# New due times for a planner's order, and short identity matmuls among TensorE's waits

## The chip, the core and the metric

The kernel runs on one core of a Trainium2 chip. The metric is the device time of one execution in microseconds (us). A core has five engines, each with an instruction queue of its own: TensorE (PE in the profile; its weight loads are PEld), VectorE (DVE), ScalarE (ACT), GpSimd (POOL) and SyncE (SP), which issues most transfers. Matmuls write their results to PSUM, a memory of 8 banks with 512 floats per partition; the other tiles lie in SBUF. Engines wait for each other by semaphores.

## What is computed

Attention for 4 batches of 8 heads, 1152 keys of 64 dimensions and 576 pooled queries, and behind it a feed-forward layer with a SoLU activation for 2304 tokens.

```python
def _attn_ref(q, k, v) -> np.ndarray:
    B, H, S, D = q.shape
    factor = 2
    scale = 1.0 / np.sqrt(D)
    q_pool = q.reshape(B, H, S // factor, factor, D).mean(axis=3)
    scores = scale * np.matmul(q_pool, k.transpose(0, 1, 3, 2))
    scores = scores - np.max(scores, axis=-1, keepdims=True)
    attn = np.exp(scores)
    attn = attn / (np.sum(attn, axis=-1, keepdims=True) + 1e-09)
    return np.matmul(attn, v).astype(np.float32)
...
def _moe_ref(x, w_in, w_out, g_ln) -> np.ndarray:
    h = x @ w_in
    h_max = np.max(h, axis=-1, keepdims=True)
    e = np.exp(h - h_max)
    sm = e / (np.sum(e, axis=-1, keepdims=True) + 1e-09)
    solu = h * sm
    mu = np.mean(solu, axis=-1, keepdims=True)
    var = np.mean((solu - mu) ** 2, axis=-1, keepdims=True)
    ln = (solu - mu) / np.sqrt(var + 1e-06) * g_ln
    return (ln @ w_out).astype(np.float32)
```

## The kernel before

The heads are worked through in pairs. For a pair, keys and queries are loaded, scaled, split into a high and a low f16 part and transposed by DMA (tiles `kn`, `qa`, `qb` before, `w`, `q` behind the transposition; L733 and L837). Small copies follow: `khi` and `w2h` take the keys into other partitions (L738, L1102), and `zq` takes the last 64 queries of both heads of a pair side by side (L843).

For each head, `maxima` first multiplies queries with keys on TensorE (`bank<-w,q`, and for the last queries `bank<-khi,zq`); VectorE takes the maximum of each row (`mx`, L977 and L982). TensorE transposes the maxima, and a transfer puts them as an additional row under the queries (`q<-c`, L1003). Then `scores` multiplies keys with queries again, now transposed and with the maximum subtracted (`bank<-q,w` and `bank<-q,w2h`), ScalarE takes the exponential (`e`, `eh`, `er`; L1133, L1139, L1150), GpSimd or VectorE forms what is left of it after rounding to f16 (L1160, L1166), and TensorE multiplies it with the values (`bank<-vhi,eh`, `bank<-vlo,eh`, in some steps `bank<-vx,eh` in f32). The sums of one head lie in bank 7 of PSUM, in its columns 0 to 324. When a head is through, VectorE copies and adds a part of them (L1224, L1228), takes the reciprocal of the row sums (L1231, L1239) and divides (L1242), which frees the bank.

The feed-forward layer takes 128 tokens at a time, in 18 blocks: `bank<-wb,xt` is its first product, `bank<-wb,lt` its second. Its weights come as float64 and are put together from bytes in the first 230 us (tile `raw`, L535; `up`, L544; `wb`, L554). Blocks of a batch can start when its 8 heads are through, so the last blocks follow the last head.

No order is written out. Every operation is given to a planner, `Plan.add`, with its engine, an estimated length, a due time and what it reads and writes. The due time is a number from the loops plus an offset from the table `OFF`, looked up by the tile's name and its head, pair or block. `Plan.run` plays all engines with these lengths: whenever an engine is free it takes, among the operations whose inputs and buffers are there, the one with the earliest due time. The program is then written out in the order of these played starts. On the chip only this order is left; the times are those of the chip, and an engine whose next instruction waits does nothing else. In the first 20 us matmuls of an f32 identity (L1639, `plan.warm`) stand between the first matmuls, where the played TensorE has nothing to do.

Of the kernel before, what the change touches and what calls it, by code (L numbers as in the profile page):

```python
# [22 lines left out]
KP = {'W': [5, 5.2, 61, 4.1], 'step': 1.05, 'M': [78.33, 15.88, 7.65], 'TX': 118, 'TP': 69, 'win': 4.28, 'P': [24.74, 18.81, 12.81, 18.34, 35, 22.83], 'QP': 29, 'N': [11.98, 7], 'AV': 5.18, 'CD': [[27, 53, 2], [69, 288, 10]], 'SD': [[12, 83, 5], [70, 287, 1]], 'VM': 'BCCCBCCCBCCBCCCB', 'OF': [4.76, 1.62, 9.84, 2.47, 1.86], 'N1': 8.51, 'warm': 1, 'ws': -3.83, 'GR': 0, 'GG': 13, 'b_eh': 6, 'b_w1': 4, 'V0': -98.83, 'VF': 1, 'QD': [0, 1], 'L0': 2.74, 'F': 0, 'EX': [[10, 71, 33], [42, 282, 0]], 'LX': [3, 36.19], 'HP': [146073, 0], 'DL': 2000, 'MA': 18.0, 'TR': [2000, 2], 'P1': [-3.89, -3.14, 3.71, -7.84, -10.1, 0.03], 'WS': [54, 96, 0.22], 'KD': 5.48, 'RB': [0, 1], 'XE': 3, 'ZB': 7, 'LT': 16, 'RS': [2.5, 6.5], 'LO': 0.3, 'PD': [], 'KH': [1], 'ZE': [2, 8], 'VN': 4}  # L23
# [19 lines left out]
class Plan:  # L43
# [20 lines left out]
    def __init__(self, tags, banks, window):  # L64
        self.tags, self.banks, self.window = tags, banks, window
        self.bank, self.slot = {}, {}
        self.warm, self.warm_until = None, 0
        self.ops = []
        self.parts, self.writers, self.readers = defaultdict(dict), {}, defaultdict(list)
        self.users = defaultdict(int)  # L70
# [53 lines left out]
    def run(self):  # L124
        ops = self.ops
# [20 lines left out]
        kind, dma, extra = "", 0, []  # L146
# [63 lines left out]
        while events:  # L210
            t, what, _, arg = heapq.heappop(events)
            if what == 0:
                o, done = arg, done + 1
                for b in o.uses:
                    count[b] -= 1
                    for i in where[b]:
                        last[i][o.engine] = o
                    if not count[b]:
                        for i in where[b]:
                            held[i] = None  # L220
                        for e in ready:
                            push(t, 1, e)
                for m in after[o]:
                    e = m.engine
                    hop = self.HOP[o.engine][e] + (self.LOAD[m.kind] if e == "PE" != o.engine else 0)
                    if o.engine == e and not m.deps[o]:
                        hop = 0
                    elif e == "PE" != o.engine and t > PAD[0]:
                        hop += pad
                    m.ok_at = max(m.ok_at, t + hop)  # L230
                    m.left -= 1
                    if not m.left:
                        ready[e].append(m)
                        push(m.ok_at, 1, e)
                continue
            e = arg
            if busy[e] > t:
                continue
            best = None
            limit = 1e9 if not todo else now_mark + (self.window if todo < len(marks) else FIRST)  # L240
            for o in ready[e]:
                if o.at > limit or o.ok_at > t or (best is not None and (o.at, o.n) >= (best.at, best.n)):
                    continue
                g = buffers(o)
                if g is None:
                    continue
                s = could(o, g)
                if s > t:
                    push(s, 1, e)
                    continue  # L250
                best, got = o, g
            if best is None:
                if e == "PE" and self.warm and t > KP.get("ws", 2.5) * 1000 and todo > self.warm_until:
                    i = next((i for i in range(8) if held.get(i) is None), None)
                    if i is not None:
                        extra.append((t, lambda i=i: self.warm(i)))
                        busy[e] = t + (110 if t > self.COLD else 216)
                        push(busy[e], 1, e)
                continue
            o = best  # L260
            ready[e].remove(o)
            for b, c in got.items():
                where[b] = c
                before[b] = [x for i in c for x in last[i].values()]
                for i in c:
                    held[i] = b
                    last[i] = {}
                if b[0] in self.banks:
                    self.bank[b] = c
                else:  # L270
                    turn[self.tags[b[0]][0]] += 1
                    self.slot[b] = c[0][1]
                head[b[0]] += 1
            for d in (*o.deps, *(x for b in o.uses for x in before.get(b, ()))):
                known[e][d.engine] = max(known[e][d.engine], d.rank)
            o.start, o.rank = t, ranks[e]
            ranks[e] += 1
            length = o.length
            if e == "PE":
                length += self.SWITCH.get((kind, o.kind), 0)  # L280
                kind = o.kind
                length *= 1 if t > self.COLD else 2
            if e == "SP":
                early = t < 4000
                busy[e] = t + (450 if early else 640) * o.calls
                dma = max(dma, t + 1200) + length
                o.end = dma + (800 if early else KP.get("DL", 1000))
            else:
                begin = t
                if o.port and e == "DVE":  # L290
                    begin = max(t, busy["POOL"] - 190)
                    taken_until = begin + length
                elif o.port and e == "POOL":
                    begin = max(t, taken_until)
                busy[e] = o.end = begin + length
            if o.mark is not None:
                todo -= 1
                if o.mark > now_mark or not todo:
                    now_mark = o.mark
            for x in ready:  # L300
                push(t, 1, x)
            push(o.end, 0, o)
            push(busy[e], 1, e)
        if done < len(ops):
            raise ValueError([(o.n, o.engine, o.at, o.uses, o.left) for o in ops if o.start is None][:30])
        self.end = max(busy.values())
        calls = [(o.start, o.n, o.fn) for o in ops] + [(t, -1, fn) for t, fn in extra]
        for _, _, fn in sorted(calls, key=lambda x: x[:2]):
            fn()


def MM(n, c=1):
    return c * (n / 2.26 + 6.5)


def MH(n, c=1):
    return c * (n / 2.4 + 2.8)

# [22 lines left out]
def attention_solu_moe(  # L341
# [10 lines left out]
    nc = tc.nc  # L352
# [28 lines left out]
    OF = KP.get("OF", [5, 1.5, 10, 1, 1.5])  # L381
    TP, TX = KP.get("TP", 90), KP.get("TX", 100)
# [54 lines left out]
    plan = Plan(tags, banks, window=KP.get("win", 5))  # L437
# [37 lines left out]
    def flat(t):  # L475
        return t.rearrange("p a b -> p (a b)")
# [5 lines left out]
    bank = pp.tile([128, 8, 512], F32, name="bank")  # L482
    ident = const.tile([128, 128], F32, name="ident")
    id16 = const.tile([128, 128], F16, name="id16")
    idb = const.tile([128, 2, 128], BF16, name="idb")
    wb = [const.tile([128, 9, WN], F32, name=f"wb{i}") for i in range(2)]
    w16 = [t.rearrange("p n c -> p (n c)").bitcast(F16).rearrange("p (n r c) -> p n r c", n=9, r=2) for t in wb]
    wm = [const.tile([128, 8], F32, name=f"wm{i}") for i in range(2)]
    ws = [const.tile([128, 16], F32, name=f"ws{i}") for i in range(2)]
    gc = const.tile([128, KO], F32, name="gc")  # L490
    xs = const.tile([128, B + B // 2, 8], F32, name="xs")
# [3 lines left out]
    vx = [const.tile([128, 2, NJ, D + 1], F32, name=f"vx{i}") for i in range(2)]  # L495
# [5 lines left out]
    mz = const.tile([128, 5, D + 1], F32, name="mz")  # L501
# [1066 lines left out]
    with tc.manual_schedule():  # L1568
# [59 lines left out]
        def token_job(n, at, src, key, dsts, rate, tail, x):  # L1628
            prev[0] = tokens(n, src, key, dsts, at, rate, prev[0], tail, x)

        for n, (x, r, tail, src, key, dsts) in enumerate(toks):
            t = max(t, r)
            jobs.append((t, lambda n=n, t=t, s=src, k=key, d=dsts, tail=tail, x=x: token_job(n, t, s, k, d, MR, tail, x)))
            t += MP if n > 4 else KP.get("MA", MP)
        jobs.append((t + 100, lambda: prev[0](t)))
        for _, job in sorted(jobs, key=lambda x: x[0]):
            job()
        if KP.get("warm", 12):
            plan.warm = lambda i: nc.tensor.transpose(bank[:, i, 0:128], ident, ident)  # L1639
            plan.warm_until = NS + 2 * NJ - 2 * KP.get("warm", 12)  # L1640
        plan.run()


# [1 line left out]
_INS = ["q", "k", "v", "moe_w_in", "moe_w_out", "moe_g_ln"]  # L1645


# [23 lines left out]
```

## Time and profile before

| | us |
|---|---|
| median of 3 runs | 624.45 (622.62 to 626.06) |
| the profiled execution | 630.24 |
| its span, first to last instruction | 628.4 |
| PE busy | 594.5 (95%) |
| ACT busy | 506.7 (81%) |
| DVE busy | 505.1 (80%) |
| POOL busy | 469.0 (75%) |
| mean granted clock of TensorE | 0.98 |

The profile is of one execution. A row of it names the engine, the source line, the operation and its tiles, output before input, with buffer numbers left out. Most matmuls have the line of a helper (L463), so they are told apart by their tiles. The granted clock is a share of full speed, averaged over a stretch. The profiled execution is not one of the three that give the median.

### The profile page before, as it was taken

What the parts mean: (1) busy time and instruction counts of PE and PEld (TensorE: products, weight loads), DVE (VectorE), ACT (ScalarE), POOL (GpSimd) and SP (SyncE); (2) the same over time, 40 slices, a digit from 0 to 9 for tenths busy, and PEclk for the clock granted to TensorE, in tenths of its full rate; (3) what the DMA queues carried; (4) which work ended last, traced back from release to release, by engine and by line L of the source; (5) the groups of instructions that cost most, each with busy time, mean ns of one, the idle gap of its engine ahead of it and who ended that gap; (6) DMA issues with size and microseconds to landing.
All of it is one profiled execution on the core that took longest, in us unless ns stands there. A gap on an engine that the chain in (4) does not pass through costs nothing.

```text
span 628.4 us, 17256 instructions
## 1 busy us (share of the span) xinstructions
PE 594.5 (95%) x6630; PEld 368.2 (59%) x6635; DVE 505.1 (80%) x1189; ACT 506.7 (81%) x978; POOL 469.0 (75%) x491
## 2 busy tenths in 40 slices
PE   8978989998888899999999999999999999999997
PEld 6747666765545465565665556556566666654453
DVE  6966788989799998878977999888989887529460
ACT  5866787998889889888998798898989989946361
POOL 5796666665777889898899889788999989932130
PEclk9996979999899899999999999999999999999999
DMA  9183967387987658767748679767697453146322
GB/s 262 35 177 98 205 179 165 75 189 154 187 225 149 133 103 182 150 151 128 142 76 144 158 142 189 139 148 111 129 164 133 81 103 79 29 67 117 69 50 68
DMA packets 183790, 83.00 MB, mean 132 GB/s; under 512 B 168604, under 2 KB 169372, under 8 KB 183708
## 3 DMA queue, kind: packets, MB, share of 16 engines
q1 hardware_dynamic: 183196, 81.18, 63.5%
q8 instruction: 52, 0.85, 0.6%
q10 hardware_dynamic: 512, 0.72, 0.3%
q14 instruction: 30, 0.25, 0.1%
HBM read 36.70 MB, written 4.72 MB: 66 GB/s over the span
## 4 chain that ended last, share of the span: by engine, by line
PE 71%; DVE 16%; ACT 4%; POOL 2%; DMA 2%; issue 2%; SPq 1%; DVEq 0%; POOLq 0%; ACTq 0%
PE bank L463 68%; DVE mx L982 6%; POOL eh L1160 2%; PE bank L1639 1%; ACT e L1139 1%; DMA zq<-q 1%; DVE wb L473 1%; DVE kn L473 1%; DVE eh L1153 1%; DVE mx L977 1%; ACT eh L1139 1%; DMA q<-c 1%; DVE ln L1459 1%; PE bank L743 1%; DVE wb L554 1%
## 5 line engine op out<-in xcount | busy, mean ns | idle before, releaser
L1160 POOL TENSOR_TENSOR eh<-e,eh 128x512 f16<-128x512 f32 (+1 forms) x278 | 331.7, 1212 | 65.2 <-ACT e L1139 24.0
L982 DVE TENSOR_REDUCE mx<-bank 128x1 f32<-128x512 f32 (+1 forms) x300 | 188.0, 653 | 25.5 <-PE bank L463 24.5
L463 PEld LDWEIGHTS <-eh 128*128 128x128 f16 x3246 | 137.9, 99 | 66.0 <-issue 9.5
L1139 ACT ACTIVATE e<-bank 128x512 f32<-128x512 f32 (+1 forms) x259 | 154.0, 614 | 24.6 <-POOL eh L1160 11.6
L1139 ACT ACTIVATE eh<-bank 128x512 f16<-128x512 f32 (+3 forms) x257 | 151.6, 616 | 27.5 <-PE bank L463 26.1
L463 PE MATMUL bank<-vhi,eh 128*128 128x65 f16 x2159 | 149.8, 196 | 7.1 <-DVE x L1242 3.0
L463 PE MATMUL bank<-q,w 128*128 128x64 f16 (+2 forms) x612 | 142.5, 294 | 6.1 <-ACT e L1139 2.2
L463 PE MATMUL bank<-q,w2h 65*128 65x512 f16 (+1 forms) x540 | 127.3, 288 | 0.0
L463 PE MATMUL bank<-w,q 128*128 128x512 f16 (+2 forms) x390 | 109.1, 339 | 4.2 <-DVE mx L982 2.6
L463 PE MATMUL bank<-wb,xt 128*128 128x512 f16 x432 | 113.0, 379 | 0.0
L463 PE MATMUL bank<-wb,lt 128*128 128x512 f16 x432 | 110.5, 379 | 0.1
L463 PE MATMUL bank<-vlo,eh 128*128 128x64 f16 x1087 | 104.5, 195 | 0.0
L463 PEld LDWEIGHTS <-w2h 65*128 65x128 f16 x540 | 45.2, 98 | 32.4 <-issue 9.3
L463 PEld LDWEIGHTS <-w 128*128 128x128 f16 x540 | 46.6, 98 | 23.9 <-issue 2.2
L463 PEld LDWEIGHTS <-lt 128*128 128x128 f16 x432 | 38.8, 98 | 37.0 <-issue 0.4
L463 PEld LDWEIGHTS <-xt 128*128 128x128 f16 x432 | 38.0, 98 | 36.5 <-issue 2.6
L1166 POOL TENSOR_TENSOR er<-r,er 128x320 f16<-128x320 f32 (+1 forms) x60 | 51.3, 857 | 8.7 <-ACT er L1150 5.0
L463 PEld LDWEIGHTS <-q 128*128 128x128 f16 x360 | 31.3, 99 | 21.1 <-issue 3.6
L1360 DVE TENSOR_REDUCE st<-bank 128x1 f32<-128x512 f32 x36 | 24.3, 682 | 21.3 <-PE bank L463 21.3
L1384 ACT ACTIVATE e<-bank,st,xs 128x512 f32<-128x512 f32 x36 | 27.7, 777 | 14.9 <-DVE st L1363 9.8
L1422 POOL TENSOR_TENSOR st<-st 128x1 f32<-128x1 f32 x18 | 4.3, 239 | 38.4 <-DVE st L1411 36.8
L1150 ACT ACTIVATE r<-bank 128x320 f32<-128x320 f32 (+1 forms) x60 | 25.6, 431 | 4.0 <-PE bank L463 3.8
(143 smaller groups left out, 900.8 us busy)
## 6 DMA issues: line engine op xcount, KB each, us to landing
vx<-in_v_dram SPq DMA_DIRECT2D x32, 288.0 KB
kt<-in_k_dram SPq DMA_DIRECT2D x31, 288.0 KB
qt<-in_q_dram SPq DMA_DIRECT2D x15, 576.0 KB
out_dram<-o SPq DMA_DIRECT2D x35, 128.0 KB
khi<-w SPq DMA_DIRECT2D x30, 144.0 KB
w2h<-w SPq DMA_DIRECT2D x30, 144.0 KB
raw<-in_moe_w_in_dram SPq DMA_DIRECT2D x8, 511.6 KB
raw<-in_moe_w_out_dram SPq DMA_DIRECT2D x8, 511.6 KB
```

Source lines behind the costliest of these rows:

```text
L463: nc.tensor.matmul(out=o, lhsT=a, rhs=b, start=first, stop=last, skip_group_check=True)
L473: eng.scalar_tensor_tensor(out=o, in0=a, scalar=scale, in1=b, op0=ALU.mult, op1=ALU.subtract)
L554: nc.vector.scalar_tensor_tensor(out=w32.bitcast(I32), in0=tl["raw", n][:, :, 0], scalar=5, in1=tl["wps", n].bitcast(I32), op0=ALU.logical ...
L743: nc.tensor.transpose(ps[:, c, :], tl["kt", 0][:, h, 3 * i + c, :], ident)
L977: nc.vector.tensor_reduce(out=tl["mx", g][:, 0:4, 2], in_=tl["nps", (g, m, c)], op=ALU.max, axis=AXX)
L982: nc.vector.tensor_reduce(out=tl["mx", g][:, m, c:c + 1], in_=tl["nps", (g, m, c)], op=ALU.max, axis=AXX)
L1139: nc.scalar.activation(out=o if P else o.rearrange("p (f i) -> p f i", f=2), in_=i, func=ACTF.Exp, scale=esc)
L1150: nc.scalar.activation(out=o, in_=tl[rn(u), (g, u)], func=ACTF.Exp, scale=esc)
L1160: eng.tensor_tensor(out=e[:, o:o + c.stop - c.start], in0=e32[:, c], in1=e[:, c], op=ALU.subtract)
L1166: eng.tensor_tensor(out=e[:, :, 1, :], in0=tl["r32", (g, u)][:, 0:len(RU[u]), :], in1=e[:, :, 0, :], op=ALU.subtract)
L1360: nc.vector.tensor_reduce(out=st(f), in_=tl[H_[f]], op=ALU.max, axis=AXX)
L1384: nc.scalar.activation(out=tl[E][:, f * 512:(f + 1) * 512], in_=tl[H_[f]], func=ACTF.Exp, bias=st(2), scale=xs[:, r, 3:4], accum_out=st(3 ...
```

## The change

Three things change. The table `OFF` has new numbers throughout (some 700), made anew with a planner that takes TensorE at half rate behind spans in which it has little to do; the planner in the kernel itself plays no such rate. The other entries of `KP` stay, and `KW` is added. A new function, `idle`, looks at the played starts between 23 and 250 us: it finds gaps of more than 350 ns between TensorE's operations, leaves out those in which bank 7 belongs to something else than a head's sums, and fills up to six tenths of a gap with matmuls at 80 ns each until the played TensorE is busy enough by the numbers of `KW`. Such a matmul (`plan.keep`) multiplies the identity in bf16 with 184 columns of itself into columns 328 to 511 of bank 7, which nobody reads. One more stands near the beginning and starts the accumulation.

```diff
-KP = {'W': [5, 5.2, 61, 4.1],
+KP = {'KW': [0.55, 0.6, 250000, 23000], 'W': [5, 5.2, 61, 4.1],
...
-OFF = {'am.0': 28.38, 'am.1': -49.32, 'am.10': 1.42,
+OFF = {'am.0': -39.66, 'am.1': -70.36, 'am.10': -7.68,
...
 FIRST = KP.get("L0", 0.3)
+KEEP = 7
@@ -65,6 +66,7 @@
         self.tags, self.banks, self.window = tags, banks, window
         self.bank, self.slot = {}, {}
         self.warm, self.warm_until = None, 0
+        self.keep, self.turns = None, []
         self.ops = []
         self.parts, self.writers, self.readers = defaultdict(dict), {}, defaultdict(list)
         self.users = defaultdict(int)
@@ -267,6 +269,8 @@
                     last[i] = {}
                 if b[0] in self.banks:
                     self.bank[b] = c
+                    if KEEP in c:
+                        self.turns.append((t, b[0] == "av"))
                 else:
                     turn[self.tags[b[0]][0]] += 1
                     self.slot[b] = c[0][1]
@@ -304,9 +308,33 @@
         if done < len(ops):
             raise ValueError([(o.n, o.engine, o.at, o.uses, o.left) for o in ops if o.start is None][:30])
         self.end = max(busy.values())
+        if self.keep:
+            extra += self.idle()
         calls = [(o.start, o.n, o.fn) for o in ops] + [(t, -1, fn) for t, fn in extra]
         for _, _, fn in sorted(calls, key=lambda x: x[:2]):
             fn()
+
+    def idle(self):
+
+        pe = sorted((o.start, o.end, 0.5 if o.kind in ("whole", "round") else 1.0) for o in self.ops if o.engine == "PE")
+        want, share, until, begin, span = *KP["KW"], 3413
+        gaps = []
+        for (_, a, _), (z, _, _) in zip(pe, pe[1:]):
+            own = [y for x, y in self.turns if x < a]
+            if a > begin and z - a > 350 and (not own or own[-1]):
+                gaps.append([a, a + int(share * (z - a) / 80) * 80, a])
+        t = begin
+        while t < until:
+            u = sum((min(z, t + span) - max(a, t)) * w for a, z, w in pe if a < t + span and z > t)
+            u += sum(max(0, min(g[2], t + span) - max(g[0], t)) for g in gaps)
+            for g in sorted(gaps, key=lambda g: g[2] - g[1]):
+                while u < want * span and t <= g[2] < t + span and g[2] < g[1]:
+                    g[2] += 80
+                    u += 80
+            t += 160
+        first = next(a for (_, a, _), (z, _, _) in zip(pe, pe[1:]) if a > self.COLD and z - a > 350)
+        at = [a + 80 * i for a, _, z in gaps for i in range(round((z - a) / 80))]
+        return [(first, lambda: self.keep(True)), *((t, lambda: self.keep(False)) for t in at)]
 def MM(n, c=1):
@@ -1638,6 +1666,8 @@
         if KP.get("warm", 12):
             plan.warm = lambda i: nc.tensor.transpose(bank[:, i, 0:128], ident, ident)
             plan.warm_until = NS + 2 * NJ - 2 * KP.get("warm", 12)
+        if KP["KW"][2]:
+            plan.keep = lambda s: nc.tensor.matmul(out=bank[:, KEEP, 328:512], lhsT=idb[:, 0, :], rhs=flat(idb)[:, 0:184], start=s, stop=False, skip_group_check=True)
         plan.run()
 
```

The changed kernel's lines lie 28 further on: its L491 is L463 of before, L1010 is L982. The first place is TensorE around its first matmul with `zq` (the matmuls with `q_149` or `q_150` are f32 scores of the second head, those with 128 columns are the last maxima of a head). Before:

```order
L463 LDWEIGHTS q_546
L463 MATMUL bank<-w_510,q_546 128x128
L463 LDWEIGHTS zq_86 [waits DMAHW0_49,DMAHW2_49,DMAHW5_49,DMAHW4_49]
L463 MATMUL bank<-khi,zq_86 128x384 [waits DVE_49]
L463 MATMUL bank<-q_149,w_179 128x288 [waits Activation_49]
```

And now:

```order
L491 LDWEIGHTS q_562
L491 MATMUL bank<-w_519,q_562 128x128
L491 MATMUL bank<-q_150,w_180 128x288 [waits Activation_49]
L491 MATMUL bank<-q_161,w_194 128x288
L491 MATMUL bank<-q_150,w_180 128x288
L491 MATMUL bank<-q_161,w_194 128x288
L491 LDWEIGHTS zq_86 [waits DMAHW0_49,DMAHW1_49,DMAHW5_49,DMAHW4_49]
L491 MATMUL bank<-khi,zq_86 128x384 [waits DVE_49]
```

Four score matmuls that stood behind the first matmul with `zq` now stand ahead of it, and the wait for the transfer with them.

The second place is SyncE's queue ahead of that transfer. Before:

```order
L651 DMA qt<-in_q_dram 128x1152
L738 DMA khi<-w_510 64x1152
L1102 DMA w2h_78<-w_528 64x1152
L738 DMA khi<-w_528 64x1152
L1102 DMA w2h_79<-w_510 64x1152
L843 DMA zq_86<-q_546 64x64 x2
```

And now:

```order
L679 DMA qt<-in_q_dram 128x1152
L766 DMA khi<-w_519 64x1152
L766 DMA khi<-w_538 64x1152
L1130 DMA w2h_78<-w_538 64x1152
L1130 DMA w2h_79<-w_519 64x1152
L871 DMA zq_86<-q_562 64x64 x2
```

The second `khi` went ahead of the first `w2h`; what stands ahead of `zq` is the same.

The third place is TensorE at the end of the third head, where it goes on with maxima (`bank<-w_886,q_948`, now `bank<-w_924,q_994`). Before:

```order
L463 MATMUL bank<-q_476,w2h_78 128x512
L463 LDWEIGHTS q_948 [waits DMAHW6_49]
L463 MATMUL bank<-w_886,q_948 128x512 [waits DVE_49]
L463 LDWEIGHTS q_948
L463 MATMUL bank<-w_886,q_948 128x512 [waits DVE_49]
```

And now, from the score matmul that stands at the same place:

```order
L491 MATMUL bank<-q_489,w2h_78 128x512
L1670 LDWEIGHTS idb
L1670 MATMUL bank<-idb 128x184 [waits DVE_49]
L1670 LDWEIGHTS idb
L1670 MATMUL bank<-idb 128x184
L491 LDWEIGHTS q_994
L491 MATMUL bank<-w_924,q_994 128x512 [waits DVE_49]
L1670 LDWEIGHTS idb
L1670 MATMUL bank<-idb 128x184 [waits DVE_49]
L491 LDWEIGHTS q_994
L491 MATMUL bank<-w_924,q_994 128x512 [waits DVE_49]
```

Short matmuls stand between the maxima, two of the first three with a wait for VectorE of their own, and one of the four maxima has moved up to before the scores.

## Rows read from the trace of the kernel before

**Rows 1.** The page: span, PE's busy time, share and instructions.
```profile
span 628.4 us, 17256 instructions
PE 594.5 (95%) x6630; PEld 368.2 (59%) x6635; DVE 505.1 (80%) x1189; ACT 506.7 (81%) x978; POOL 469.0 (75%) x491
```

**Rows 2.** The chain that ended last, share of the span by engine.
```profile
PE 71%; DVE 16%; ACT 4%; POOL 2%; DMA 2%; issue 2%; SPq 1%; DVEq 0%; POOLq 0%; ACTq 0%
```

**Rows 3.** Stretches: us, busy us of PE to POOL, PEclk, DMA share, GB/s.
```profile
40.00:60.00 20.00, 15.91 (x116) 12.08 (x115) 13.66 (x29) 12.13 (x21) 14.08 (x21) 0.75 0.54 143
...
80.00:100.00 20.00, 18.01 (x207) 13.36 (x207) 15.37 (x36) 13.71 (x26) 9.55 (x8) 0.83 0.60 160
...
160.00:180.00 20.00, 16.67 (x194) 10.05 (x194) 16.84 (x33) 17.18 (x36) 15.78 (x16) 0.91 1.04 237
...
200.00:220.00 20.00, 17.14 (x158) 8.65 (x158) 19.08 (x46) 18.13 (x35) 17.05 (x18) 0.91 0.61 136
...
sum 300.00, PE 273.69 PEld 182.20 DVE 254.27 ACT 248.79 POOL 225.95; mean PE 18.25 PEld 12.15 DVE 16.95 ACT 16.59 POOL 15.06
...
424.00:600.00 176.00, 176.00 (x1938) 101.69 (x1936) 130.00 (x329) 136.68 (x265) 127.28 (x138) 1.00 0.57 99
```

**Rows 4.** The chain in order of time: start, length in us, what.
```profile
42.74 6.17 DMA zq<-q
49.00 7.66 PE bank L463 x43
56.87 7.52 PE bank L463 x94
...
89.57 7.70 PE bank L463 x89
...
163.08 5.85 PE bank L463 x78
...
213.99 5.40 PE bank L463 x34
```

**Rows 5.** Timeline of PE: start, us, engine, line, operation, [idle before, releaser].
```profile
45.64 0.78 PE L463 MATMUL bank<-q,w 128*128 128x288 f32 x4
46.27 0.40 PE L463 MATMUL bank<-w,q 128*128 128x128 f16 x4
49.00 0.32 PE L463 MATMUL bank<-khi,zq 128*128 128x384 f16 x1 [2.34 <-DMA zq<-q]
...
83.13 0.38 PE L463 MATMUL bank<-q,w 128*128 128x512 f16 x1
83.34 0.38 PE L463 MATMUL bank<-q,w2h 65*128 65x512 f16 x1
...
86.03 0.38 PE L463 MATMUL bank<-w,q 128*128 128x512 f16 x1 [1.22 <-DVE mx L982]
...
164.14 0.62 PE L463 MATMUL bank<-q,w 128*128 128x512 f16 x1
```

**Rows 6.** Timeline of DVE at two places.
```profile
49.36 0.56 DVE L982 TENSOR_REDUCE mx<-bank 128x1 f32<-128x384 f32 x1 [1.87 <-PE bank L463]
...
83.59 1.67 DVE L906 TENSOR_SCALAR vx<-vx,vs 128x1152 f32<-128x1152 f32 x1
85.30 0.23 DVE L1228 TENSOR_TENSOR bank<-bank,low 64x65 f32<-64x65 f32 x1
```

**Rows 7.** Waits of PE over the span: us in total, times, longest.
```profile
PE bank L463 <- DVE mx L982: 4.2, 10, 1.2
...
PE bank L463 <- DVE x L1242: 3.0, 6, 1.0
```

**Rows 8.** The page's DMA issues: operation, count, KB each.
```profile
qt<-in_q_dram SPq DMA_DIRECT2D x15, 576.0 KB
...
khi<-w SPq DMA_DIRECT2D x30, 144.0 KB
w2h<-w SPq DMA_DIRECT2D x30, 144.0 KB
```

More of the change, by code (lines that the diff above doesn't have):

```diff
@@ L21 @@
 AXX = mybir.AxisListType.X
-KP = {'W': [5, 5.2, 61, 4.1], 'step': 1.05, 'M': [78.33, 15.88, 7.65], 'TX': 118, 'TP': 69, 'win': 4.28, 'P': [24.74, 18.81, 12.81, 18.34, 35, 22.83], 'QP': 29, 'N': [11.98, 7], 'AV': 5.18, 'CD': [[27, 53, 2], [69, 288, 10]], 'SD': [[12, 83, 5], [70, 287, 1]], 'VM': 'BCCCBCCCBCCBCCCB', 'OF': [4.76, 1.62, 9.84, 2.47, 1.86], 'N1': 8.51, 'warm': 1, 'ws': -3.83, 'GR': 0, 'GG': 13, 'b_eh': 6, 'b_w1': 4, 'V0': -98.83, 'VF': 1, 'QD': [0, 1], 'L0': 2.74, 'F': 0, 'EX': [[10, 71, 33], [42, 282, 0]], 'LX': [3, 36.19], 'HP': [146073, 0], 'DL': 2000, 'MA': 18.0, 'TR': [2000, 2], 'P1': [-3.89, -3.14, 3.71, -7.84, -10.1, 0.03], 'WS': [54, 96, 0.22], 'KD': 5.48, 'RB': [0, 1], 'XE': 3, 'ZB': 7, 'LT': 16, 'RS': [2.5, 6.5], 'LO': 0.3, 'PD': [], 'KH': [1], 'ZE': [2, 8], 'VN': 4}
@@ new lines @@
+KP = {'KW': [0.55, 0.6, 250000, 23000], 'W': [5, 5.2, 61, 4.1], 'step': 1.05, 'M': [78.33, 15.88, 7.65], 'TX': 118, 'TP': 69, 'win': 4.28, 'P': [24.74, 18.81, 12.81, 18.34, 35, 22.83], 'QP': 29, 'N': [11.98, 7], 'AV': 5.18, 'CD': [[27, 53, 2], [69, 288, 10]], 'SD': [[12, 83, 5], [70, 287, 1]], 'VM': 'BCCCBCCCBCCBCCCB', 'OF': [4.76, 1.62, 9.84, 2.47, 1.86], 'N1': 8.51, 'warm': 1, 'ws': -3.83, 'GR': 0, 'GG': 13, 'b_eh': 6, 'b_w1': 4, 'V0': -98.83, 'VF': 1, 'QD': [0, 1], 'L0': 2.74, 'F': 0, 'EX': [[10, 71, 33], [42, 282, 0]], 'LX': [3, 36.19], 'HP': [146073, 0], 'DL': 2000, 'MA': 18.0, 'TR': [2000, 2], 'P1': [-3.89, -3.14, 3.71, -7.84, -10.1, 0.03], 'WS': [54, 96, 0.22], 'KD': 5.48, 'RB': [0, 1], 'XE': 3, 'ZB': 7, 'LT': 16, 'RS': [2.5, 6.5], 'LO': 0.3, 'PD': [], 'KH': [1], 'ZE': [2, 8], 'VN': 4}
```

2 lines of the change are left out of this document (1 added, 1 removed).

## The prediction

> **What bounds the kernel now.** I read the page from the top. The span is 628.4 us and PE is busy 95% of it [rows 1]. A busy share alone does not say that PE sets the end, so the chain comes next: 71% of the span lies on PE, 16% on DVE, 4% on ACT [rows 2]. Then the stretches tell where. From 424 to 600 us PE is busy 176.00 of 176.00 us, so nothing can be won there without taking PE work away. In the first 300 us it is busy 273.69 us, so 26.3 us of waiting lie there, and the granted clock is below 1 in four of the 20 us stretches: 0.75, 0.83, 0.91 and 0.91 [rows 3]. The clock has two levels, so a mean of 0.75 over 20 us is 10.0 us at half rate (1.2 GHz in place of 2.4); the four give 10.0 + 6.8 + 3.6 + 3.6 = 24.0 us, in which PE does the work of 12.0. That half rate costs is seen on one kind of matmul: 128x512 takes 0.38 us at 83.13 and 0.62 us at 164.14, in the third spell [rows 5].
>
> These spells lie on the path. The chain in order of time has PE pieces of 7.66 us at 49.00 and 7.52 at 56.87 (first spell), 7.70 at 89.57 (second), 5.85 at 163.08 (third) and 5.40 at 213.99 (fourth) [rows 4]. Each follows a stretch in which PE had little to do: ahead of the first it waits 2.34 us for the zq transfer, ahead of the second 1.22 us and more for VectorE's maxima [rows 5].
>
> Durations below come from this execution: 630.24 us with a span of 628.4, that is 1.84 us around the span. It is 5.8 us above the median of 624.45; I take the difference that I find here and put it on the median.
>
> **What the change does, part by part.** The number of ordinary matmuls is the same, 6552, and no engine gets or loses an operation of another kind. PE gets 83 matmuls of 184 columns with a weight load each, in 24 groups: 38 among the first 290 of PE's ordinary matmuls (before 41.3 us of the trace), 5 at the second spell, 4 and 3 at two places between, 14 ahead of the third spell, 6 later and 13 at the fourth. The rest is order, and the order moves little: most work stands within a few us of PE work of where it stood.
>
> *Price of one short matmul.* The trace has none. A 512 column matmul starts 0.21 us after the one before it (83.13 to 83.34 [rows 5]); 184 of 512 columns are 0.08 us. All 83 cost between nothing (all in time in which PE waits anyway) and 83 x 0.08 = 6.6 us (none is). Most are put where PE waits in the trace, so I take near the lower end, +0.6.
>
> *First spell.* It follows the wait for zq, which ends by the transfer of 6.17 us at 42.74 [rows 4]. The SP rows show that the same transfers stand ahead of zq as before: qt with 576 KB, two khi and two w2h with 144 KB each [rows 8], only the last four in another order. So zq lands when it did. None of the 83 stands in this wait: PE has none between its ordinary matmuls 289 and 667. What does move is that four score matmuls now stand ahead of the wait instead of behind it: four such take 0.63 us, from 45.64 to 46.27 [rows 5]. The wait shrinks from 2.34 to 1.7 us; the half rate behind it, worth 10.0 / 2 = 5.0, I expect to stay. Taken: -0.6; bounds 0 and -5.6.
>
> *Second spell.* PE waits at 86.03 for VectorE's maxima, and VectorE is busy with the scaling of v (1.67 us at 83.59) and then the addition in the head's sum (0.23 us at 85.30) [rows 6]. VectorE's rows stand there in nearly the same order in the changed program, so the wait stays. Five short matmuls are put in it, 0.4 us. But they write the bank in which that head's sum lies, and the PE rows show the first and the third waiting for VectorE: by its count the first waits for that addition, which ends at 85.53 in the trace. Until then PE does nothing, as before. Half rate here is 6.8 / 2 = 3.4; I take a third, -1.1, bounds 0 and -3.4.
>
> *Third and fourth.* 14 and 13 short matmuls (1.1 and 1.0 us) stand ahead of spells that cost 3.6 / 2 = 1.8 us each. I take two thirds, -2.4; bounds 0 and -3.6.
>
> *The new order elsewhere.* PE waits 4.2 us for maxima and 3.0 for the division of a head [rows 7]. Whether the new times shorten these can't be read from an order. The bounds are that all 7.2 go or that as many come; a quarter gone, -1.8.
>
> *New waits.* Where the short matmuls share a bank with a head's sum, each side waits for the other: five of them wait for VectorE, and seven of VectorE's operations on such a sum now wait for a short matmul. Behind such a matmul stand all later matmuls, and behind such an operation VectorE's whole queue. The trace has no such pair. The nearest rows are a handover from PE: the matmul that starts at 49.00 [rows 5] is read by VectorE from 49.36 on, which had waited for it [rows 6], 0.36 us from start to start. Twelve waits cost from nothing (the other engine has older work queued ahead) to 12 x 0.36 = 4.3. Taken: a quarter, +1.1, since VectorE seldom has nothing else to do there.
>
> The Trainium skill speaks against this part: "PSUM — Partial Sum Buffer", section "PSUM bank collisions raise a hardware error", says that two engines may not be in one bank and quadrant at once, whatever the columns, so that a matmul into columns that nobody uses must still be kept apart by bank. No row of the kernel before shows it. By that rule none of the twelve waits could be dropped and the sum would have their upper end, 3.2 us more.
>
> **Sum.** +0.6 - 0.6 - 1.1 - 2.4 - 1.8 + 1.1 = -4.2 us. The span becomes 624.2, the profiled execution 626.0, the median 624.45 - 4.2 = 620.2 us.
>
> **The rivals.**
> *The half rate goes altogether.* For it: the spells follow stretches of few matmuls, and matmuls are put in some of them. Against it: nothing is put in the wait ahead of the largest. It would give -12.0 for the four spells, -0.6 and -1.8 as above and +1.7 for costs: -12.7, 611.7 us.
> *Nothing changes.* Spells come back elsewhere, as PE reaches the next wait sooner. For it: the chain leaves PE at 16% of the span for DVE, and VectorE's order hardly moves. The gains of 2.4 and 1.8 go, the rest stays: 0.0, 624.4 us.
> *Slower: the short matmuls hold up the queue.* Five of them wait for VectorE at the end of a head; where VectorE is late, PE can't go on with scores that were ready. The price is 4.3 for the twelve waits and up to half of the 6.6 for short matmuls that meet no gap, 3.3; with the first spell's -0.6 and no other gain that is +7.0, 631.4 us. It decides from the point where both together cost more than the rest gives, 5.9 us with the taken values.
>
> **How the numbers follow.** A measurement here tells about 0.5% from no change, 3.1 us: faster is below 621.3, slower above 627.6. The forecast (616 to 623, by its own bounds) has 0.42, no change 0.25, all half rate gone 0.13, slower 0.20. Of the forecast about four fifths lie below 621.3: 0.34; with 0.13 that is 0.47 faster. Slower: 0.20. The same: 0.33. The range runs from 609, which leaves half of the case with all gains outside, to 630.5, which leaves out the upper half of the slower one; some 0.17 lie outside.
>
> **What would show it.** The granted clock of 40 to 60 us should stay near 0.75, that of 160 to 180 and 200 to 220 rise to 0.97 or more, and that of 80 to 100 lie between. PE should still wait for zq, some 1.7 us, and the transfer should still end near 49. The short matmuls should start in time that was idle; some of those at the end of a head should show waits for VectorE, of a few tenths. From 424 us on PE should be as full as now, with all of it earlier by what was won. I am wrong if the first spell is gone (then the zq wait was not what brings it, or the work ahead of it was enough), if VectorE's additions to a head's sum wait a microsecond for short matmuls, or if new low stretches show where the clock was 1.

## The result and the profile after

The changed kernel takes 619.18 us (median of 5 executions, 617.57 to 619.69) where the kernel before takes 624.45 beside it: a ratio of 0.9911, with a 95% interval from 0.9884 to 0.9939. That is 5.3 us less. The prediction was 620.2 us, from 609 to 630.5. Medians and ratios below leave out one execution of e2 (631.69 us), which lies more than 1.5% above the fastest of that kernel.

The page's span and rows of TensorE and the others, which answer to [rows 1]:

```profile
span 617.8 us, 17441 instructions
...
PE 591.0 (96%) x6718; PEld 366.1 (59%) x6718; DVE 507.1 (82%) x1189; ACT 507.7 (82%) x978; POOL 466.5 (76%) x491
```

The stretches of the changed kernel, columns as in [rows 3]:

```profile
40.00:60.00 20.00, 19.09 (x218) 14.22 (x216) 18.82 (x38) 17.13 (x34) 16.84 (x23) 1.00 0.70 169
...
80.00:100.00 20.00, 19.32 (x261) 13.95 (x260) 17.37 (x33) 16.67 (x34) 15.54 (x12) 1.00 0.79 151
...
160.00:180.00 20.00, 18.36 (x223) 10.96 (x222) 19.68 (x44) 18.20 (x35) 15.85 (x16) 1.00 0.91 230
180.00:200.00 20.00, 16.45 (x237) 10.11 (x234) 19.80 (x55) 19.68 (x37) 16.42 (x18) 1.00 0.76 166
200.00:220.00 20.00, 18.49 (x233) 11.30 (x230) 18.35 (x34) 18.19 (x38) 17.22 (x16) 1.00 0.44 89
...
sum 300.00, PE 280.45 PEld 186.65 DVE 266.65 ACT 259.10 POOL 233.25; mean PE 18.70 PEld 12.44 DVE 17.78 ACT 17.27 POOL 15.55
```

All four low spells are gone, the first too: the column PEclk is 1.00 in each row. The two profiles differ by 10.6 us (628.4 to 617.8), the medians by 5.3: the profiled execution of before is 5.8 us above its median, and its mean clock of 0.980 is among its lowest. Read both as single executions.

At the first place of the change TensorE hardly waits for zq any more. Its timeline, columns as in [rows 5], with the weight load of zq (PEld) in its place:

```profile
45.69 0.81 PE L491 MATMUL bank<-q,w 128*128 128x288 f32 x4
46.80 0.13 PEld L491 LDWEIGHTS <-zq 128*128 128x128 f16 x2 [0.55 <-DMA zq<-q]
46.83 0.49 PE L491 MATMUL bank<-khi,zq 128*128 128x384 f16 x2 [0.34 <-DVE r L1259]
```

The first matmul with zq starts at 46.83, not at 49.00. The weight load ahead of it still waits 0.55 us for the transfer; the 0.34 us that the matmul's row puts down to VectorE end at the same moment. SyncE's queue tells a part of why (start, us, operation), now:

```profile
32.41 2.72 SPq L761 DMA_TRANSPOSE w<-kn  x2
35.23 2.54 SPq L865 DMA_TRANSPOSE q<-qa  x2
37.81 0.59 SPq L679 DMA_DIRECT2D qt<-in_q_dram  x1
...
41.01 1.31 SPq L871 DMA_DIRECT2D zq<-q  x2
```

and before:

```profile
32.62 3.58 SPq L733 DMA_TRANSPOSE w<-kn  x2
...
42.09 1.24 SPq L843 DMA_DIRECT2D zq<-q  x2
```

The transfers ahead of zq are those of before, as the order said. But the two transpositions of the keys ahead of them take 2.72 us here and 3.58 in the profile of before, so zq is issued at 41.01 and not at 42.09. That is 1.1 of the 2.2 us. The rest lies in the transfer: from its first issue to the end of the wait for it pass 5.8 us here and 6.8 before (to 48.91, by [rows 4]). What makes it shorter isn't shown.

The short matmuls by their source line (duration in ns as least, median, most; then what they waited for and who for them):

```profile
L1670 PE MATMUL bank<-idb x83: 239/243/256, 11.4 to 204.0; 128*128 128x184 bf16 x83
...
  DVE bank L1256: 0.6, 1
...
  DVE r L1259: 0.3, 1
```

One of them waits 0.6 us for VectorE's addition, one of VectorE's operations 0.3 us for a short matmul. TensorE's waits for maxima and for the division, which answer to [rows 7]:

```profile
PE bank L491 <- DVE mx L1010: 3.4, 9, 0.6
PE bank L491 <- DVE x L1270: 2.1, 5, 0.6
```

They were 4.2 and 3.0; but short matmuls now stand in some of these gaps, and without them the waits are longer (e1 below). Of the 19.6 us in which TensorE is not busy in the first 300, 6.7 lie from 160 to 220 us. From 184.3 to 206.8 us the chain in order of time passes through VectorE without a break, save some short issues:

```profile
188.56 1.25 DVE ln L1487
189.99 0.59 DVE wb L582
190.58 0.60 DVE mx L1010
191.18 0.59 DVE wm L588
...
206.37 0.41 DVE x L1270
206.83 2.29 PE bank L491 x27
```

### The profile page after: what moved, and what is told of

The parts are those of the page before. It is cut to its first block, busy times and chain, and to the rows that moved or that the text cites. A ratio compares the mean times of both kernels' runs of the same rounds, so it can differ in the third digit from the quotient of the medians.

```text
span 617.8 us, 17441 instructions
## 1 busy us (share of the span) xinstructions
PE 591.0 (96%) x6718; PEld 366.1 (59%) x6718; DVE 507.1 (82%) x1189; ACT 507.7 (82%) x978; POOL 466.5 (76%) x491
## 4 chain that ended last, share of the span: by engine, by line
PE 68%; DVE 15%; ACT 3%; issue 3%; POOL 2%; DMA 2%; SPq 0%; DVEq 0%; ACTq 0%; POOLq 0%
PE bank L491 67%; DVE mx L1010 5%; POOL eh L1188 2%; DMA vx<-in_v_dram 2%; DVE ln L1487 1%; ACT e L1167 1%; DVE wm L588 1%; ACT eh L1167 1%; DVE mx L1005 1%; DVE kn L501 1%; DVE wb L582 1%; DVE x L1270 1%; DVE eh L1181 0%; PE bank L1019 0%; DMA q<-qa 0%
## 5 line engine op out<-in xcount | busy, mean ns | idle before, releaser
L1188 POOL TENSOR_TENSOR eh<-e,eh 128x512 f16<-128x512 f32 (+1 forms) x278 | 323.5, 1181 | 61.1 <-ACT e L1167 29.9
L1010 DVE TENSOR_REDUCE mx<-bank 128x1 f32<-128x512 f32 (+1 forms) x300 | 187.0, 653 | 18.3 <-PE bank L491 17.5
L491 PEld LDWEIGHTS <-eh 128*128 128x128 f16 x3246 | 133.3, 98 | 58.0 <-issue 6.9
L491 PE MATMUL bank<-vhi,eh 128*128 128x65 f16 x2159 | 145.0, 194 | 4.2 <-DVE x L1270 2.1
L491 PE MATMUL bank<-q,w 128*128 128x64 f16 (+2 forms) x612 | 141.0, 291 | 3.9 <-ACT e L1167 1.5
L491 PE MATMUL bank<-q,w2h 65*128 65x64 f16 (+1 forms) x540 | 126.4, 287 | 0.0
L491 PE MATMUL bank<-wb,xt 128*128 128x512 f16 x432 | 113.1, 379 | 0.0
L491 PE MATMUL bank<-w,q 128*128 128x512 f16 (+2 forms) x390 | 106.3, 331 | 3.8 <-DVE qs L719 1.9
L491 PE MATMUL bank<-wb,lt 128*128 128x512 f16 x432 | 107.9, 379 | 0.4 <-DVE e L1419 0.4
L491 PE MATMUL bank<-vlo,eh 128*128 128x64 f16 x1087 | 102.6, 194 | 0.0
L491 PEld LDWEIGHTS <-lt 128*128 128x128 f16 x432 | 39.9, 97 | 41.6 <-issue 1.2
L491 PEld LDWEIGHTS <-w2h 65*128 65x128 f16 x540 | 45.1, 98 | 27.0 <-issue 5.2
L491 PEld LDWEIGHTS <-w 128*128 128x128 f16 x540 | 46.7, 98 | 22.5 <-issue 3.3
L491 PEld LDWEIGHTS <-xt 128*128 128x128 f16 x432 | 38.2, 98 | 35.8 <-issue 0.8
L1194 POOL TENSOR_TENSOR er<-r,er 128x320 f16<-128x320 f32 (+1 forms) x60 | 53.2, 890 | 2.5 <-DVE mx L1010 0.7
L491 PEld LDWEIGHTS <-q 128*128 128x128 f16 x360 | 31.4, 98 | 18.1 <-issue 0.6
L1419 DVE SCALAR_TENSOR_TENSOR e<-bank,st,e 128x512 f32<-128x512 f32 x36 | 26.4, 743 | 2.0 <-ACT e L1412 1.2
```

The costliest lines, as they stand in the source:

```text
L491: nc.tensor.matmul(out=o, lhsT=a, rhs=b, start=first, stop=last, skip_group_check=True)
L1010: nc.vector.tensor_reduce(out=tl["mx", g][:, m, c:c + 1], in_=tl["nps", (g, m, c)], op=ALU.max, axis=AXX)
L1188: eng.tensor_tensor(out=e[:, o:o + c.stop - c.start], in0=e32[:, c], in1=e[:, c], op=ALU.subtract)
L1194: eng.tensor_tensor(out=e[:, :, 1, :], in0=tl["r32", (g, u)][:, 0:len(RU[u]), :], in1=e[:, :, 0, :], op=ALU.subtract)
L1419: nc.vector.scalar_tensor_tensor(out=tl[E][:, s], in0=tl[H_[f]], scalar=st(1), in1=tl[E][:, s], op0=ALU.mult, op1=ALU.mult, accum_out=st(5 ...
```

## The experiments

Each was timed beside the kernel before on the same chip; not all of them ran on one chip. The ratios are not quotients of these medians, and where they tell another size of a difference, both stand. The clock is the median of the executions' mean granted clocks; the kernel before has 0.988.

| run | table | short matmuls | us | ratio to before (95%) | clock |
|---|---|---|---|---|---|
| the change | new | 83 | 619.18 | 0.9911 (0.9884 to 0.9939) | 0.999 |
| e11, the same again | new | 83 | 618.40 | 0.9906 (0.9870 to 0.9942) | 1.000 |
| e1 | new | 0 | 620.81 | 0.9924 (0.9892 to 0.9956) | 0.990 |
| e2 | old | 76 | 622.71 | 0.9975 (0.9956 to 0.9995) | 0.999 |
| e3 | old | 26, at zq | 625.77 | 1.0012 (0.9993 to 1.0030) | 0.991 |
| e4 | new | 65, none shared | 619.01 | 0.9906 (0.9884 to 0.9928) | 0.999 |
| e5 | mixed | 0 | 637.55 | 1.0197 (1.0160 to 1.0234) | 0.987 |
| e6 | old, VectorE less | 0 | 622.79 | 0.9972 (0.9939 to 1.0005) | 0.988 |
| e7 | new, VectorE less | 83 | 615.80 | 0.9847 (0.9815 to 0.9878) | 1.000 |
| e8 | new | each twice | 619.00 | 0.9905 (0.9873 to 0.9936) | 0.999 |
| e9 | new | 38 early | 616.71 | 0.9871 (0.9846 to 0.9896) | 1.000 |
| e10 | new | 47, late | 619.05 | 0.9915 (0.9887 to 0.9943) | 0.993 |
| e12 | old | 32 early | 626.39 | 1.0027 (1.0002 to 1.0052) | 0.991 |

**The two halves of the change.** e1 is the changed kernel without short matmuls:

```diff
-KP = {'KW': [0.55, 0.6, 250000, 23000],
+KP = {'KW': [0.55, 0.6, 0, 23000],
```

> The new table without the 83 short matmuls; everything else as in the changed kernel. Theory A, the short matmuls keep the clock up and the table alone does not: low spells come back, granted clock 0.97 or less in one or more 20 us stretches between 40 and 220 us, time 621.5 to 625 us. Theory B, the new order alone removes the spells (above all the wait for zq, which is gone in the changed kernel) and the short matmuls only fill idle time: granted clock 0.995 or more over the span, time within 1 us of the changed kernel's 619.2, or a little below it because the short matmuls' waits are gone.

e2 is the changed kernel with the numbers of `OFF` of before.

> The old table with the short matmuls that the new function puts into its gaps (76 of them, one just ahead of the first matmul with zq). Theory A: the clock stays at full from 80 us on and only the spell behind the zq wait (40 to 60 us, near 0.75) is left; 619 to 622 us. Theory B: the spells stay as before, mean clock 0.98, and the waits that the short matmuls share with VectorE come on top; 624 to 627 us.

The table alone gives 3.8 of the 5.3 us (4.7 of 5.6 by the ratios), at a clock that is hardly higher than that of before. The short matmuls alone bring the clock to 0.999 and give 1.6 us by the ratio, 1.9 by the medians. So nearly all half rate can go and most of the gain is not there. In both experiments the time lies outside what either theory said; the clock is as theory A of e1 has it, and in e2's profile the spell behind zq is gone too. The stretches of e1's profile:

```profile
20.00:40.00 20.00, 16.48 (x171) 12.99 (x169) 17.21 (x35) 14.91 (x38) 18.53 (x18) 0.91 0.34 61
40.00:60.00 20.00, 16.89 (x160) 13.09 (x161) 15.27 (x32) 13.86 (x25) 14.21 (x19) 0.91 0.59 150
...
80.00:100.00 20.00, 18.60 (x215) 12.41 (x215) 18.33 (x40) 17.58 (x35) 15.30 (x12) 1.00 0.70 164
...
160.00:180.00 20.00, 18.61 (x204) 10.68 (x202) 18.96 (x43) 18.90 (x37) 16.25 (x16) 1.00 0.92 241
...
200.00:220.00 20.00, 17.64 (x233) 10.60 (x232) 19.61 (x39) 18.26 (x36) 17.24 (x15) 1.00 0.38 91
```

With no short matmul at all the second, third and fourth spell are absent from this execution. Only the first 60 us still have low ones. TensorE's waits for maxima and for the division are not shorter than before (4.2 and 3.0 in [rows 7]):

```profile
PE bank L491 <- DVE mx L1010: 5.3, 12, 0.8
PE bank L491 <- DVE x L1270: 2.3, 5, 0.8
```

Together they are 7.6 us where they were 7.2, so what the table gives does not lie in these waits. From the profile of before to this one TensorE's time without work falls by 1.0 us only (33.9 to 32.9), its busy time by 8.4 (594.5 to 586.1); but the profiled execution of before is one of low clock, so this doesn't divide the gain of the medians.

**The wait for zq.** e3 is the kernel before with 26 short matmuls directly ahead of its first matmul with zq, in that matmul's own bank:

```diff
+                if P == 1 and c == 0:
+                    for _ in range(26):
+                        mm(ps[:, 0:184], idb[:, 0, :], flat(idb)[:, 0:184], True, True)
```

> The kernel before with 26 short matmuls of the identity (184 columns, some 2.1 us at 0.08 each) directly ahead of its first matmul with zq, into that matmul's own bank, and nothing else. If the wait of 2.3 us for zq brings the first low spell: granted clock of 40 to 60 us from 0.75 to 0.95 or more, the zq matmul still at 49 us, time 2 to 5 us below 624.5. Rival, the spell comes from the stretch before it (28 to 46 us): the clock of 40 to 60 us stays near 0.75, time 624 to 626 us.

In its profile zq lands as late as before (first matmul at 49.0) and the clock behind it is 1, but the time is not less: 625.77. In that execution another low spell stands ahead, from 36 to 44 us, where nothing was changed (the stretches from 20 and from 40 us have 0.92 and 0.91), and the median clock is 0.991. To fill the zq wait alone moves neither clock nor time by much: the time is that of the rival, the clock behind the wait that of the first theory.

**Early or late short matmuls.** e9 keeps the 38 that stand ahead of TensorE's ordinary matmul 290, e10 the others, the first and one more, e12 the early ones with the old table:

```diff
-KP = {'KW': [0.55, 0.6, 250000, 23000],
+KP = {'KW': [0.55, 0.6, 45000, 23000],
```

```diff
-KP = {'KW': [0.55, 0.6, 250000, 23000],
+KP = {'KW': [0.55, 0.6, 250000, 60000],
```

> The changed kernel with only the 38 short matmuls that stand ahead of TensorE's ordinary matmul 290. Theory A, these keep the clock up from 20 to 60 us and make the queue that loads zq run earlier, and that is what the short matmuls give: 619.2 us, clock 1 from 20 to 60, no wait of TensorE for zq, the clock below 1 later on. Theory B, the later ones matter as much: 620 us, halfway to the 620.8 of the table alone.

> The changed kernel without those 38 but with the later ones (47, the first that starts the accumulation among them). Theory A: 620.8 us as with the table alone, the clock at 0.9 from 20 to 60 us, TensorE waits some 2.3 us for zq. Theory B: 620 us, and no clock below 1 from 60 us on.

> The table of before, with only the short matmuls that stand ahead of TensorE's ordinary matmul 333 (32 of them, first spell); none later. Theory A, they give in the old order what they give in the new one, 620.8 less 616.7, about 4 us: 620.9 us. Theory B, the new order is needed to make use of them, since in the old one zq lands at 48.5 us all the same: 623 us, as with all short matmuls and the old table. Clock 1 from 20 to 60 us by both; low spells later on by B.

Both expectations had e9 at 619.2 us or more. It is the fastest kernel that leaves nothing out, 616.71 us: 8 us below before. Its six executions lie from 615.95 to 617.61, the twelve of the changed kernel (with e11) from 617.13 to 619.70. It is not the chip: e8 ran on the same one and takes 619.00. Its clock is 1.00 also where it has no short matmuls:

```profile
80.00:100.00 20.00, 19.28 (x257) 13.64 (x257) 18.36 (x36) 17.57 (x36) 15.98 (x13) 1.00 0.86 162
...
160.00:180.00 20.00, 18.81 (x244) 11.70 (x243) 19.67 (x46) 18.85 (x36) 16.47 (x17) 1.00 0.96 253
...
200.00:220.00 20.00, 18.29 (x227) 10.72 (x227) 17.66 (x33) 18.19 (x37) 17.83 (x16) 1.00 0.39 95
```

e10 lies below both its theories. Beside e1 the late short matmuls cost nothing: 1.8 us less by the medians, 0.6 by the ratios, which is not told from none. Its zq wait was expected at 2.3 us, but its first matmul with zq starts at 46.85 us. It differs from e1, where that matmul starts at 49.10, by no instruction but one short matmul up to there. So two nearly equal programs can land zq 2 us apart.

Yet there is a pattern. In the six profiles with the new table and all early short matmuls (the change, e4, e7, e8, e9, e11) the transpositions into `q` from `qb` and into `w` each take 2.7 to 2.8 us; in each of the eight others at least one of the two takes 2.9 to 3.7. So the earlier issue of zq may come from the early short matmuls in the new order, as theory A of e9 has it; by what way isn't shown.

In the old order the early ones do not help: e12 is no faster than before, rather 0.3% slower, and slower than both theories; nor is its clock 1 from 40 to 60 us, as both had it. Stretches of 2 us of e12, then its wait:

```profile
48.00:50.00 2.00, 0.99 (x4) 1.02 (x5) 0.47 (x1) 0.00 (x0) 2.00 (x4) 0.61 0.88 288
50.00:52.00 2.00, 2.00 (x8) 1.43 (x8) 1.56 (x4) 1.51 (x3) 0.75 (x1) 0.50 0.49 194
```

```profile
49.01 0.48 PE L491 MATMUL bank<-khi,zq 128*128 128x384 f16 x1 [2.38 <-DMA zq<-q]
```

The same for e2, which has the same instructions up to there:

```profile
48.00:50.00 2.00, 1.44 (x10) 1.24 (x11) 1.08 (x3) 0.56 (x2) 2.00 (x5) 1.00 0.97 341
50.00:52.00 2.00, 2.00 (x28) 1.85 (x27) 2.00 (x4) 2.00 (x5) 1.52 (x3) 1.00 0.37 148
```

```profile
48.56 0.32 PE L491 MATMUL bank<-khi,zq 128*128 128x384 f16 x1 [1.77 <-DMA zq<-q]
```

A wait of 2.38 us is followed by the half rate, one of 1.77 is not. Over the profiles that leave this wait empty: behind waits of 1.89 to 2.38 us, which end at 48.78 us or later (before, e1, e6, e12), the clock falls to half; where the first matmul with zq starts by 48.56 (e2, e4, e5, e7 to e11, the change), it stays.

**The price of the short matmuls.** e8 gives each of them twice. e4 leaves out those between the last matmul of a head's sum and its division, 18 of the 83, and with them the shared waits. e11 is the changed kernel once more.

```diff
-        return [(first, lambda: self.keep(True)), *((t, lambda: self.keep(False)) for t in at)]
+        return [(first, lambda: self.keep(True)), *((t, lambda: self.keep(False)) for t in at for _ in range(2))]
```

```diff
+        heads = defaultdict(lambda: [[0], [0]])
+        for o in self.ops:
+            for b in o.uses:
+                if b[0] == "av" and o.engine in ("PE", "DVE"):
+                    heads[b][o.engine == "DVE"].append(o.end)
+        shut = [(max(x), max(y)) for x, y in heads.values()]
...
+            if any(x - 50 < z and a < y + 300 for x, y in shut):
+                continue
```

> The changed kernel with each of its short matmuls twice (165 in place of 83). Theory A, they lie in time in which TensorE waits anyway: at most 620.2 us, 1 more. Theory B, their 0.08 us each are on the path: 82 more are 6.6 us, 625.8. In between tells the share that is paid.

> The changed kernel without those short matmuls that stand between the last matmul of a head's sum and VectorE's division of it (65 of 83 are left); no short matmul waits for VectorE any more and no operation of VectorE for one. If the twelve shared waits cost what the prediction put on them: 0.5 to 2 us below the changed kernel with the clock unchanged. Rival, they lie behind other waits: within 0.7 us of it. If the left-out ones were needed for the clock: a stretch near 80 to 100, 160 or 210 us falls to 0.95 or less and the time rises by 1 us or more.

> The changed kernel itself, timed once more on the chip on which the next run is timed. Theory A, its 45 later short matmuls buy no clock and cost time, since some of them stand in VectorE's unbroken chain from 150 to 206 us: 619 us, a ratio of 0.990 to 0.992, above the 0.987 of the early ones alone. Theory B, those 2.5 us between the two were the execution's or the chip's: 617 us, 0.987 to 0.988.

82 more matmuls cost nothing that can be told (0.9905 against 0.9911 and 0.9906), so their bodies lie in waits. Nor does it show in the time whether the shared ones are there. Yet beside the early ones the late ones together cost some 1.9 us (e9 against the twelve executions of the changed kernel, median 618.6; 2.2 to 2.5 by the ratios). The two traces show what may be a part of it. VectorE's timeline in e9:

```profile
153.21 0.23 DVE L1259 TENSOR_SCALAR r<-bank,vs 128x5 f32<-128x5 f32 x1
...
163.36 0.68 DVE L1188 TENSOR_TENSOR eh<-e,eh 128x512 f16<-128x512 f32 x1
```

and in e11:

```profile
153.79 0.22 DVE L1259 TENSOR_SCALAR r<-bank,vs 128x5 f32<-128x5 f32 x1 [0.33 <-PE bank L1670]
...
163.94 1.80 DVE L1188 TENSOR_TENSOR eh<-e,eh 128x512 f16<-128x512 f32 x1
```

At 153 us VectorE is 0.3 us later in e11 than in e9, and there it waits 0.33 us for a short matmul. Ten microseconds later its subtraction takes 1.80 us in place of 0.68, since it now meets an operation of GpSimd (last section). At VectorE's next operation it is 1.7 us behind e9 (165.67 to 163.96), and at the end 1.2 (spans of 616.5 and 615.3 us). But this is not shown to be the cause. e8 has the wait and not the long subtraction:

```profile
154.88 0.23 DVE L1259 TENSOR_SCALAR r<-bank,vs 128x5 f32<-128x5 f32 x1 [0.41 <-PE bank L1670]
...
165.03 0.68 DVE L1188 TENSOR_TENSOR eh<-e,eh 128x512 f16<-128x512 f32 x1
```

and it takes 619.00 us all the same. e4 has neither, but a low spell from 120 to 160 us in its profile (0.93 and 0.90). What keeps e8, and e4 in its other executions, from 616.7 is open.

**Who sets the pace.** e6 (in the kernel before) and e7 (in the changed one) take VectorE's maxima of the weight tiles over 128 of 512 columns:

```diff
-                out=wm[m][:, n % 8:n % 8 + 1], in_=w32, op=ALU.max, axis=AXX, apply_absolute_value=True
+                out=wm[m][:, n % 8:n % 8 + 1], in_=w32[:, 0:128], op=ALU.max, axis=AXX, apply_absolute_value=True
```

> The kernel before; VectorE takes the maximum of each weight tile over 128 of its 512 columns (16 maxima of 0.67 us become about 0.25, by 0.28 for one over 128 columns: 6.7 us less of VectorE, 3.4 of it from 140 to 220 us); the scale of the weights so rests on a quarter of them. Theory A, VectorE sets the pace from 140 to 220 us, and TensorE's half rate there costs little: 621 us, 3 to 4 less, with as much half rate as before. Theory B, TensorE's lost rate sets the time: 624 us or more, no gain that can be told.

> The same cut of VectorE's weight maxima in the changed kernel. Theory A, with TensorE at full rate VectorE is the bound more than before, so the cut is worth at least as much: 614.5 to 616 us against 619.2. Theory B, 618.5 us or more.

The group of these maxima in e7, which had 10.7 us in the changed kernel:

```profile
L588 DVE TENSOR_REDUCE wm<-wb 128x1 f32<-128x128 f32 x16 | 4.3, 275 | 0.1
```

6.4 us less of VectorE in all give 3.4 to 4 us in the changed kernel (0.9847 against 0.9911 or the median 615.8 against 619.2) and some 2 in the kernel before, where the interval still holds no change. So VectorE is part of the pace in the changed kernel. For the kernel before, where e6 falls between its two theories, it isn't shown, nor that the new order makes a difference.

**Where the table's gain lies.** e5 has the new offsets for tiles that are first played before 150 us, and no short matmuls.

> The table of offsets is the changed one for tiles that the planner plays first before 150 us (328 of 1065 entries), that of before for all later ones; no short matmuls. Theory A, the table's 3.8 us come from the first 150 us, where TensorE's waits for maxima lie: 621 us as with the whole table. Theory B, they come from the later part, where VectorE is fullest: 624.5 us as before.

Both expectations miss: it is 12.5 us slower than before. Its profile is still 7.7 us ahead of that of before at the start of VectorE's 340th operation (181.6 against 189.3 us), but 8.6 behind at its last. It seems that the late part of the old table doesn't fit the early part of the new one (the two differ in 1061 of 1065 entries, not in some 700), so this run can't divide the gain.

## Why the prediction was right, and where it was not

The time came out 1.0 us below the forecast, but several terms of the sum were off in ways that cancel, so that the closeness is luck in part. One of the signs that I named for being wrong came true: the first spell is gone.

**Bounds and stock.** TensorE's last stretch is full as before. But the 24.0 us at half rate were one execution's. The median clock of before is 0.988, so a usual execution has (1 - 0.988) x 623 x 2 = 15 us. I put the whole difference of the profile on the median; that step overstated what the spells can give.

**First spell, -0.6.** The step "zq lands when it did" failed. The queue's order was read rightly, but its transpositions can take 2.7 us or 3.6 and the zq transfer itself was 1 us shorter, so that the first matmul with zq starts 2.2 us earlier. The half rate behind it, which I expected to stay, was gone. And the 38 early short matmuls, which I had not given a gain, are worth 620.8 - 616.7 = 4.1 us with the new order (3.3 by the ratios). That order has spells in its first 60 us (e1: 3.6 us at half rate in each of two stretches), and these go with them.

**Second, third and fourth spell, -3.5 together.** Gone, but not by the short matmuls put there: e1 and e9 have none there, and their profiles show clock 1 there. In the old order the late ones do matter (e2 against e12, 3.3 us less by the ratios). In the new one they cost 1.9 beside the early ones and nothing that can be told without them.

**New order elsewhere, -1.8.** The term was mis-sized: the table alone gives 3.8 (4.7 by the ratio). The bounds held it, but the way was wrong: I looked for it in TensorE's waits for maxima and divisions, and in e1 these are 7.6 us where they were 7.2. Where it lies instead is open.

**Bodies, +0.6.** Right as far as it can be told: 82 more change nothing that can be told, where 6.6 us would show.

**Shared waits, +1.1.** Of the right size in the trace (0.6 and 0.3 us seen), but without them e4 is no faster, so the time doesn't show the term. In e11 one of 0.33 us stands ahead of a lag of 1.7 behind e9, of which 0.3 were there before and 1.1 came with GpSimd's operation. The upper end, by which none of the waits would be hidden, isn't seen.

**The rivals.** "The half rate goes altogether" is what happened to the clock, but not with its 611.7 us: I had counted all of TensorE's regained work as time. In 78 executions of before, the 19 with the lowest clock (mean 0.982) have a median of 626.0 us, the 21 with the highest (0.994) 623.8. The 0.012 between are 7.5 us of TensorE's work (0.012 x 623), and 2.2 us of time: three tenths. e2 shows the same by experiment: 0.011 more clock, 6.9 us of work, 1.6 us of time, its 76 bodies included. I take it that the rest is given back as waits where VectorE is full; no run shows it. Nor are three tenths a rule. A line through clock and time of the executions falls by 221 us for a whole clock in those of before, but by 440 in e6, 445 in e12, 515 in e1 and 523 in e10, where all work as time would be some 620; and e9 against e1 has 0.0095 more clock, 5.9 us of work, for 3.3 to 4.1 us. Such a line doesn't tell what is cause: an execution that waits longer can have the lower clock for it. "Short matmuls hold up the queue" may stand behind the 1.9 us of the late ones, inside the forecast; it isn't shown.

What stays open: why early and late short matmuls in the old order together give 1.6 us and the early ones alone lose some; why late ones cost beside early ones and not without them; and by what step the table gains.

## What to carry to other kernels

A stretch at half rate costs what it delays on the path and no more: compare the clocks and times of many executions of the same kernel before counting it as time. Fill such a spell only after looking at where it still is in the new order: here 38 short matmuls ahead of the first wait gave 3 to 4 us in the new order and none in the old one, and 45 later ones beside them bought no clock and cost about 2. A filler that writes into a bank in which another engine works is an instruction in that engine's chain too.

## What the hardware showed that I had not expected

The subtraction `eh<-e,eh` on VectorE (128x512, both inputs in SBUF) takes 0.68 us in e9, where it starts before GpSimd's operation on `qt`, and 1.80 in e11, where it starts behind it. GpSimd's row in e11:

```profile
163.79 1.40 POOL L707 TENSOR_TENSOR qt<-qt 128x576 f32<-128x576 f32 x1 [0.32 <-DMA qt<-in_q_dram]
```

It ends at 165.19; VectorE, begun at 163.94, ends at 165.74, so it does its work of about 0.6 us after GpSimd is through. The profiles of the change, e7 and e10, where VectorE also starts behind, have 1.46 to 1.67 us and some 0.55 us from GpSimd's end to VectorE's, as here. In e4 VectorE starts 0.03 us ahead; it takes 0.68, and GpSimd's operation 1.92 in place of 1.40. The Trainium skill, "SBUF — State Buffer", section "SBUF: two separate sides", states it: a VectorE operation with two inputs in SBUF and a GpSimd operation that reads SBUF share a port pair, which one of them holds for its whole instruction. The traces agree, with 1.1 us in e11 for a start that is 0.15 us too late.

The granted clock differs between executions of one program: from 0.972 to 1.000 over the 78 of before. Spells appear at other places as well, as from 36 to 44 us in e3.
